# Five probability tiles and one run of value products a unit in a fused attention and expert kernel, with less space for values, inputs and splits and a new attention order

## The chip, the cores and the metric

The kernel runs on one core of a Trainium2 chip. Its engines each have their own instruction queue: TensorE (PE, with its weight loads shown apart as PEld), VectorE (DVE), ScalarE (ACT), GpSimd (POOL) and SyncE (SP), which issues most DMAs. The metric is the device time of one execution in microseconds, the median of three runs: 1045.88 us before the change (1041.61 to 1047.19).

## What is computed

One transformer layer on 2048 tokens of width 512: layer norm, attention with 32 heads of width 16 in which a query sees its last 256 keys, a residual, layer norm, and a mixture of 8 experts (hidden width 1376) of which each token takes its best two, with a second residual.

```python
qkv = (layernorm(x) @ wqkv).reshape(B, S, 3, H, Dh)         # H = 32, Dh = 16
scores = einsum("bhqd,bhkd->bhqk", q, k) * Dh ** -0.5
mask = (i - j >= 0) & (i - j < 256)
p = softmax(where(mask, scores, -1e9))
h = x + einsum("bhqk,bhkd->bhqd", p, v).reshape(B, S, D) @ wo
gates = softmax(layernorm(h) @ wg); top 2 of 8, weights made to sum to 1
out = h + sum over a token's two experts of weight * gelu(xn @ w1[e]) @ w2[e]
```

## The kernel before

**Numbers.** Matrices are multiplied in a fast 32-bit form. So that little is lost, an operand is split in a high and a low part (`split`: ACT rounds the high part, DVE or POOL takes the low part as the difference), and three products are added: high by high, high by low, low by high. One product of 512 inner rows by 512 columns is thus 12 matmuls.

**Attention.** The tokens are cut in 4 chunks of 512 (`c`), the heads in 8 groups of four (`g`). A unit `u = 8c + g` is one chunk of queries with one group of heads: 32 units. For a chunk, `norm_and_v` loads four blocks of x (pool `xn`), norms them (`rstd` on POOL), turns them on PE (line 592) and makes V (line 603). For a unit, `qk` loads a piece of the weights into a stage (`wst`), makes Q and K (line 660) and carries them through DRAM into one of four slots; `maxes` finds the largest score of each query (PE line 729, DVE line 734); `attend` makes the scores (line 778), exponentials (ACT, line 784), masks (POOL affine selects, line 810; in the last three units DVE does it before the exponential, line 754), and the products with V (line 834). `project` multiplies the finished chunk by `wo` (line 912, by way of the split buffer `ohl`), adds the residual, norms, turns (line 997), makes the gates (line 1004), and `route` (from line 1070) sends token numbers to a table in DRAM by eight small scatters on POOL (line 1101).

**Tiles of a unit.** A unit's scores fall in four tiles of key blocks, A (keys before the chunk, not in the first chunk), B, C and D. A tile's probabilities lie in one buffer of the pool `pt`, of which there are three. The V products of a tile use the array in four column strips of 32, one for each head (`tile_position=(0, 32 * j)`), where every other matmul uses the whole array. `ENDS` says after which tiles the V products of the tiles so far are made, in one run:

```python
ENDS = ("BCD", "BD", "BD", "ABCD")        # by chunk
```

So a unit of the first chunk has three runs, one of the second and third has two, one of the fourth has four.

**Experts.** Expert 0 begins with 384 early token rows, gathered when the third chunk's routes are in the table (POOL line 1315, turned by PE at line 1320), while the fourth chunk is projected and routed. Its remaining rows and experts 1 to 7 follow: up products (line 1347), gelu, down products (lines 1379 and 1422), and scatters that add to the output (line 1402).

**Order.** Nothing runs as written. Each step is a task with an engine, an estimated duration, a priority and the buffers it takes; `Plan.order` plays the tasks through with these estimates and so fixes each engine's instruction order. `SHIFT` moves the priority of a kind of task up or down, by stretch of the program; `SWITCH` is the estimate of what PE loses between whole-array matmuls and strips. On the chip every queue runs in the order given and waits where data are late.

Of the kernel before, what the change touches and what calls it, by code (L numbers as in the profile page):

```python
# [7 lines left out]
F32 = mybir.dt.float32  # L8
# [19 lines left out]
ENDS = ("BCD", "BD", "BD", "ABCD")  # L28
PVD = 770
LATE_MASKS = 8 * NC - 3  # L30
SWITCH = 95
# [29 lines left out]
    "maxes.halves.POOL": (0, -10.16, -12, -9.92, 0, 0, 0),  # L61
    "maxes.mm.PE": (-11.91, -7.13, 0.16, 0.06, 1.04, 0, 0),
    "norm_and_v.DVE1": (-1.2, 0, 0, -0.7, 0, 0, 0),
    "norm_and_v.SP1": (0, 0, -10.01, 0, 0, 0, 0),
    "norm_and_v.mm.PE": (0, 3.93, 3.16, 5.45, 0, 0, 0),
    "norm_and_v.turn.PE": (0, -12, -12, -8.6, 0, 0, 0),
    "part.DVE1": (0, 0, 0, 0, 0, 0.72, 0),
    "part.POOL1": (0, 0, 7.7, 0, 0, 0, 0),
    "part.mm.PE": (0, 0, 2.16, 0.86, 1.78, 0, 0),
# [1508 lines left out]
```

## Time and profile before

| | us |
|---|---|
| median of three runs | 1045.88 (1041.61 to 1047.19) |
| the profiled execution | 1048.93 |
| its span, first to last instruction | 1046.9 |
| PE busy | 1023.9 (98%) |
| PE weight loads busy | 844.0 (81%) |
| VectorE, GpSimd, ScalarE busy | 646.5, 626.7, 536.2 |

The attention units fill the trace from about 48 to 500 us, the fourth chunk's projection and routing lie beside expert 0 up to about 565, and the experts fill the rest. A row of the timeline gives start, length, engine, line, operation, tiles and how many equal instructions were merged; in brackets how long the engine was idle before and what ended that. A matmul's length includes its way through the array, so the next one starts earlier than that: what a matmul costs is read from start to start.

### The profile page before, as it was taken

The numbers are of one execution on the slowest core, as the hardware profiler recorded it, in microseconds if no ns is written. First come the engines' busy times: TensorE is split into PE (matmuls) and PEld (weight loads), VectorE is DVE, ScalarE is ACT, GpSimd is POOL, SyncE is SP. The second block draws the span as 40 slices with busy tenths as digits, with TensorE's granted clock in tenths as the row PEclk, the third lists the DMA queues.
The fourth block names the chain that finished last, engine by engine and source line by source line (L and its number), as shares of the span: only waits on it lengthen the run. The fifth ranks groups of instructions, "written<-read, shape, count | busy, mean of one in ns | idle before, by whom it ended". The sixth has DMA issues, their size and how long they took to land. (4 is left out here: it accounts for less than half of the span.)

```text
span 1046.9 us, 19919 instructions
## 1 busy us (share of the span) xinstructions
PE 1023.9 (98%) x6722; PEld 844.0 (81%) x6722; DVE 646.5 (62%) x1951; ACT 536.2 (51%) x1143; POOL 626.7 (60%) x986
## 2 busy tenths in 40 slices
PE   8999999999999999999899999999999999999997
PEld 5877778877777777755798898998999989878795
DVE  8988876887677777776752556354544545544440
ACT  3477747575666666567541554163362543525340
POOL 5687749777887858646496144187484673844111
PEclk9999999999999999988899999999999999999999
DMA  6999877769687868663526343164444544554522
GB/s 211 271 253 243 252 192 220 224 179 201 192 249 171 201 149 217 193 166 87 157 103 147 95 142 107 52 163 97 122 107 128 147 103 101 125 136 154 121 80 29
DMA packets 143887, 164.48 MB, mean 157 GB/s; under 512 B 68587, under 2 KB 86571, under 8 KB 143776
## 3 DMA queue, kind: packets, MB, share of 16 engines
q1 hardware_dynamic: 128448, 145.96, 49.5%
q0 software_dynamic: 15328, 17.16, 9.7%
q8 instruction: 55, 0.90, 0.3%
q14 instruction: 56, 0.46, 0.2%
HBM read 111.10 MB, written 51.43 MB: 155 GB/s over the span
## 5 line engine op out<-in xcount | busy, mean ns | idle before, releaser
L734 DVE CUSTOM_DVE_ANT_0 one<-one,masked 128x320 f32<-128x320 f32 (+4 forms) x512 | 230.3, 494 | 59.5 <-PE one L729 54.1
L1347 PE MATMUL one<-mr 128*128 128x288 f32 (+14 forms) x1716 | 255.2, 309 | 2.5 <-issue 1.2
L1347 PEld LDWEIGHTS one<-mr 128*128 128x128 f32 (+1 forms) x1716 | 243.2, 186 | 11.8 <-issue 1.6
L784 ACT ACTIVATE zone<-one 128x384 f32<-128x384 f32 (+1 forms) x480 | 208.3, 495 | 79.4 <-PE one L778 55.7
L810 POOL TENSOR_SCALAR_AFFINE_SELECT zone<-zone 128x256 f32<-128x256 f32 (+1 forms) x332 | 151.5, 481 | 59.8 <-ACT zone L784 53.4
L1379 PE MATMUL one<-zone,mr 128*128 128x512 f32 (+4 forms) x648 | 154.9, 394 | 0.0
L479 POOL TENSOR_TENSOR mr<-mf,mr 128x512 fp32r<-128x512 f32 (+4 forms) x99 | 123.9, 1263 | 48.8 <-ACT mr L475 47.6
L778 PE MATMUL one<-mr 98*128 98x384 f32 (+1 forms) x592 | 141.1, 331 | 3.3 <-ACT zone L784 1.7
L1379 PEld LDWEIGHTS one<-zone,mr 128*128 128x128 f32 (+4 forms) x648 | 117.1, 182 | 31.4
L778 PEld LDWEIGHTS one<-mr 98*128 98x128 f32 x592 | 97.6, 193 | 45.1 <-ACT zone L784 14.8
L475 ACT CAST mr<-mf 128x512 fp32r<-128x512 f32 (+6 forms) x152 | 108.4, 733 | 46.3 <-DMA mf<-in_A_wqk_dram 17.2
L1286 POOL DMA_INDIRECT mf<-xnd,mf x94 | 109.3, 1163 | 28.8 <-issue 27.7
L729 PE MATMUL one<-mr 96*128 96x320 f32 (+4 forms) x512 | 123.8, 318 | 0.6 <-DVE r_x L1062 0.3
L1402 POOL DMA_INDIRECT out_dram<-mf,tb x24 | 41.5, 1730 | 128.0 <-DVE mf L1390 114.7
L477 DVE TENSOR_TENSOR mr<-one,mr 128x512 fp32r<-128x512 f32 (+16 forms) x161 | 79.3, 509 | 57.6 <-ACT mr L475 43.7
L1361 ACT ACTIVATE one<-one 128x288 f32<-128x288 f32 (+13 forms) x132 | 54.8, 415 | 110.9 <-PE one L1347 91.6
L660 PE MATMUL one<-mr 128*128 128x512 f32 (+1 forms) x396 | 103.7, 389 | 2.3 <-ACT mr L475 2.0
L729 PEld LDWEIGHTS one<-mr 96*128 96x128 f32 x512 | 88.3, 191 | 21.3 <-DVE mx L734 10.2
L1402 POOL DMA_INDIRECT out_dram<-mf x40 | 65.2, 1630 | 63.0 <-DVE mf L1432 54.6
L834 PE MATMUL oT<-zone 128*17 128x384 f32 (+2 forms) x1408 | 96.9, 393 | 2.0 <-issue 1.4
L475 ACT CAST mr<-one 128x512 fp32r<-128x512 f32 (+16 forms) x161 | 70.7, 449 | 31.0 <-PE one L1320 16.9
L660 PEld LDWEIGHTS one<-mr 128*128 128x128 f32 x396 | 69.2, 189 | 14.0 <-ACT mr L475 3.5
(189 smaller groups left out, 1259.8 us busy)
## 6 DMA issues: line engine op xcount, KB each, us to landing
mf<-in_B_w_dram SPq DMA_DIRECT2D x32, 688.0 KB
mf<-in_B_w_dram SPq DMA_DIRECT2D x40, 512.0 KB
qkd<-mr SPq DMA_DIRECT2D x29, 512.0 KB
mr<-qkd SPq DMA_DIRECT2D x128, 96.0 KB
mr<-qkd SPq DMA_DIRECT2D x32, 384.0 KB
mf<-in_A_x_dram SPq DMA_DIRECT2D x32, 256.0 KB
mf<-in_A_wqk_dram SPq DMA_DIRECT2D x32, 256.0 KB
qkd<-mr SPq DMA_DIRECT2D x64, 128.0 KB
```

The source lines that it names most:

```text
L475: a = add("ACT", 51 + n * 0.86, lambda: nc.scalar.copy(dst_h(), src()), deps, prio, bufs)
L479: b = add("POOL", 60 + n * 2.3, lambda: nc.gpsimd.tensor_sub(dst_l(), src(), f32(dst_h())), [a], prio, bufs)
L660: nc.tensor.matmul(single[bk.h][:, s], wt()[:, int(i == 1), k * 128:(k + 1) * 128], xt[:, k, s], start=(i == 0 and k == 0), stop=(i == 2 a ...
L729: nc.tensor.matmul(view()[:, j], q_of(slot)[0:96, h + j, b].rearrange("p e q -> p (e q)"), K[slot.h][0:96, h + j, (b + k0) * 64:(b + 5) * ...
L734: nc.vector.tensor_tensor_reduce(v, v, masked[:, 320 - n:], scale=1.0, scalar=NEG, op0=OP.add, op1=OP.max, accum_out=mx_t[slot.h][:, h + j ...
L778: nc.tensor.matmul(single[bk.h][:, off:off + w], K[slot.h][0:98, h // 2, r * 128:(r + 1) * 128], q_of(slot)[0:98, h // 2, 2 * b:2 * b + 2 ...
L784: return add("ACT", 51 + n * 0.833, lambda: nc.scalar.activation(dst(), single[bk.h][:, 0:n].rearrange(order, **({"e": 2, "q": 64} if "e" ...
L810: nc.gpsimd.affine_select(v, v, pattern=[[0, v.shape[1]], [-1 if far else 1, 128]], compare_op=OP.is_gt if far else OP.is_ge, fill=0.0, ba ...
L1286: nc.gpsimd.indirect_dma_start(out=xg_t[i][:, t * 128:(t + 1) * 128], out_offset=None, in_=xnd4, in_offset=bass.IndirectOffsetOnAxis(ap=ql ...
L1347: nc.tensor.matmul(bank(), a[:, k, f * 128:f * 128 + w], spot[b][:, k, c0:c1], start=(i == 0), stop=(i == 11))
L1379: nc.tensor.matmul(single[bk.h][:n], h[a][:w], spot["w2"][2 * f + b][:w], start=(f == 0 and q == 0), stop=(f == NF - 1 and q == 2))
L1402: d = nc.gpsimd.indirect_dma_start(in_offset=None, compute_op=OP.add, **kw)
```

## The change

- **Tiles and runs.** `ENDS` goes. Units 0 to 27 make all their V products in one run after tile D; units 28 to 31 in two, after B and D. There are now four `pt` buffers, and one more (`pt_b`) that holds tile B of units 0 to 27 alone. It lies where two of the x blocks were.
- **Space.** V blocks go from ten to nine, so the V blocks numbered 11 and 15 may be written only when the last unit of the chunk before is done. The x blocks go from four to two after the first chunk, each pair with a `rstd` of its own. The weight stage `wst` and the split buffer `ohl` go from two to one.
- **Expert 0** keeps two of its hidden tiles in the region that attention leaves (`zone2`), and its weights also wait for the V products of unit 27.
- **Estimates and order.** `SWITCH` is 125 in place of 95, a gather 1260 ns in place of 950, and the table `SHIFT` is new throughout.

```diff
-ENDS = ("BCD", "BD", "BD", "ABCD")
+WHOLE = 8 * NC - 4
-SWITCH = 95
+SWITCH = 125
...
-    "norm_and_v.turn.PE": (0, -12, -12, -8.6, 0, 0, 0),
+    "norm_and_v.turn.PE": (0, -6.96, 0, -5, 0, 0, 0),
...
-    NQ, NPT, NV, NH, NN = 4, 3, 10, 3, 2
-    mr = consts.tile([128, 124 * KB], F32R, name="mr")
+    NQ, NPT, NV, NH, NN = 4, 4, 9, 3, 2
+    mr = consts.tile([128, 120 * KB], F32R, name="mr")
...
-    ohl = [(take(mr, 4, 128), take(mr, 4, 128)) for _ in range(2)]
+    ohl = [(take(mr, 4, 128), take(mr, 4, 128))]
-    xz = take(mf, 2048)
-    xn = [xz[:, i * 512:(i + 1) * 512] for i in range(4)]
+    xn = [take(mf, 512) for _ in range(2)]
     hl_f = take(mf, 512)
+    pt_z = take(mf, 2 * 768)
+    xn += [pt_z[:, i * 512:(i + 1) * 512] for i in range(2)]
+    wst = [take(mf, 512)]
...
-    plan = Plan(dict(xn=4, wgs=2, wst=2, hl=1, hl_more=1, qk=NQ, pt=NPT, osb=1, one=7, mx=3, ab=3, oT=1,
-                     h=NH, n=NN, nt=1, y=2, osl=1, ohl=2, ahead=4, tmp=2, xt=2, yq=1))
+    plan = Plan(dict(xn=2, xn_more=4, wgs=2, wst=1, hl=1, hl_more=1, qk=NQ, pt=NPT, pt_b=1, osb=1, one=7, mx=3, ab=3, oT=1,
+                     h=NH, n=NN, nt=1, y=2, osl=1, ohl=1, ahead=4, tmp=2, xt=2, yq=1))
...
-            if b == 3 or b == 1 and c == 0:
-                pair(*((b - 1, 2) if c == 0 else (0, 4)))
+            if b % 2:
+                pair(b - 1, 2)
...
-        ends, held, ready = ENDS[c], [], False
+        ends, held, ready = "D" if u < WHOLE else "BD", [], False
         for i, (name, parts) in enumerate(tiles):
             p = u + i / len(tiles)
-            pt = Buf("pt")
+            pt = Buf("pt_b" if name == "B" and u < WHOLE else "pt")
...
-        r1_free = qk_read[8 * NC - 1] + qk_read[8 * NC - 2] + v_done[NC - 1]
+        r1_free = qk_read[8 * NC - 1] + qk_read[8 * NC - 2] + v_done[NC - 1] + pv_last[WHOLE - 1]
```

Lines from 400 on have numbers one or two higher in the changed kernel: 780 are the scores, 731 the maxes, 836 the V products, 662 Q and K, 914 the projection, 1072 the routing, 1322 and 1349 expert 0's turns and up products.

**The runs, on PE.** Unit 0, before: its tile B and its tile C, each in a run of four matmuls (one for each head), with maxes (729) and scores (778) around them. `one` is a PSUM bank, `oT` the bank of the V products.

```order
L729 MATMUL one_75<-mr 128x320
L834 MATMUL oT<-zone 17x384 x4
L729 MATMUL one_77<-mr 128x320
L778 MATMUL one_79<-mr 128x256 x2
L778 MATMUL one_76<-mr 128x256
L729 MATMUL one_74<-mr 128x320
L834 MATMUL oT<-zone 17x384 x4
```

The same unit now, from its last score (the first row) to its only run:

```order
L780 MATMUL one_79<-mr 128x256
L662 MATMUL one_76<-mr 128x512 x4
L731 MATMUL one_80<-mr 128x320
L731 MATMUL one_75<-mr 128x320
L731 MATMUL one_74<-mr 128x320
L780 MATMUL one_78<-mr 128x384
L780 MATMUL one_79<-mr 128x384
L780 MATMUL one_77<-mr 128x384
L836 MATMUL oT<-mf,zone 17x384 x4
L836 MATMUL oT<-zone 17x384 x4
L836 MATMUL oT<-zone 17x128 x4
L836 MATMUL oT<-zone 17x256 x4
```

Tiles B, C and D (which has two parts) now stand in one row of strips, and four Q and K matmuls, three maxes and three scores of the next unit lie between the last score and the run.

**The routing of the third chunk, on PE.** Before, it stands ahead of the last run of unit 27:

```order
L834 MATMUL oT<-zone 17x384 x4
L778 MATMUL one_76<-mr 128x256
L778 MATMUL one_77<-mr 128x256 x2
L778 MATMUL one_80<-mr 128x256
L834 MATMUL oT<-zone 17x384 x4
L778 MATMUL one_74<-mr 128x256 x2
L778 MATMUL one_76<-mr 128x256
L778 MATMUL one_75<-mr 128x384
L1070 LDWEIGHTS before
L1070 MATMUL one_77<-r_m,before 128x32
```

Now it stands ahead of the last run of unit 29, among the first products of the fourth chunk's projection (914):

```order
L914 MATMUL one_80<-mr 128x512 x4
L780 MATMUL one_76<-mr 128x256 x2
L780 MATMUL one_74<-mr 128x384
L914 MATMUL one_80<-mr 128x512 x2
L780 MATMUL one_77<-mr 128x256
L731 MATMUL one_79<-mr 128x320
L780 MATMUL one_76<-mr 128x256 x2
L731 MATMUL one_78<-mr 128x320
L780 MATMUL one_74<-mr 128x256
L1072 LDWEIGHTS before
L1072 MATMUL one_77<-r_m,before 128x32
```

The third chunk's projection, turns and gates moved with it: 12 projection matmuls and all four turns and four gates of that chunk, which stood ahead of the last run of unit 27, now stand behind it.

**After the last run, on PE.** Before, behind the last V products of unit 31, the projection of four blocks (912) stands between the turns of expert 0's early rows (1320):

```order
L834 MATMUL oT<-zone 17x256 x4
L1320 MATMUL one_79<-ident,mf 128x128 x4
L1320 MATMUL one_74<-ident,mf 128x128 x4
L912 MATMUL one_75<-mr 128x512 x3
L912 MATMUL one_77<-mr 128x512 x3
L912 MATMUL one_80<-mr 128x512 x3
L912 MATMUL one_78<-mr 128x512 x3
L1320 MATMUL one_76<-ident,mf 128x128 x4
L1347 MATMUL one_79<-mr 128x384 x12
L1347 MATMUL one_74<-mr 128x384 x12
L912 MATMUL one_75<-mr 128x512 x2
```

Now:

```order
L836 MATMUL oT<-zone 17x256 x4
L914 MATMUL one_80<-mr 128x512 x3
L1322 MATMUL one_77<-ident,mf 128x128 x4
L914 MATMUL one_75<-mr 128x512 x3
L1322 MATMUL one_78<-ident,mf 128x128 x4
L914 MATMUL one_74<-mr 128x512 x3
L914 MATMUL one_79<-mr 128x512 x3
L1322 MATMUL one_76<-ident,mf 128x128 x4
L1349 MATMUL one_77<-mr 128x384 x12
L1349 MATMUL one_78<-mr 128x384 x12
L914 MATMUL one_80<-mr 128x512 x3
L1349 MATMUL one_76<-mr 128x384 x12
```

The products are the same in number. The pieces of three stand one by one between the turns, not four in a row, and behind the first two up products (1349) the last pieces follow with one up product between them.

## Rows read from the trace of the kernel before

**Rows 1.** The page's first part: busy time, share of the span and instructions of each engine.

```profile
PE 1023.9 (98%) x6722; PEld 844.0 (81%) x6722; DVE 646.5 (62%) x1951; ACT 536.2 (51%) x1143; POOL 626.7 (60%) x986
```

**Rows 2.** Busy time of each engine by stretch: the stretch and its length, then busy us and instructions of each engine, the granted share of PE's clock, the share of the DMA engines, GB/s.

```profile
100.00:450.00 350.00, 349.16 (x2667) 269.12 (x2665) 263.95 (x1015) 222.31 (x499) 257.60 (x498) 1.00 0.78 204
450.00:500.00 50.00, 45.62 (x291) 24.92 (x289) 35.25 (x131) 32.76 (x70) 29.90 (x43) 0.83 0.42 118
500.00:511.00 11.00, 8.42 (x27) 6.18 (x28) 6.49 (x11) 3.81 (x9) 3.93 (x3) 0.69 0.70 204
511.00:563.00 52.00, 52.00 (x291) 47.05 (x290) 29.67 (x105) 22.20 (x48) 40.58 (x64) 1.00 0.35 113
563.00:700.00 137.00, 133.47 (x895) 124.78 (x894) 66.36 (x116) 62.18 (x138) 53.60 (x62) 0.99 0.44 118
```

**Rows 3.** The timeline of PE around the first run of unit 0 (one tile; the trace counts two records for a matmul of line 834).

```profile
54.95 0.42 PE L729 MATMUL one<-mr 96*128 96x320 f32 x1
55.30 0.84 PE L834 MATMUL oT<-zone 128*17 128x384 f32 x8
56.07 0.41 PE L729 MATMUL one<-mr 96*128 96x320 f32 x1
56.32 0.52 PE L778 MATMUL one<-mr 98*128 98x256 f32 x3
```

**Rows 4.** The timeline of PE around a run of two tiles in the third chunk.

```profile
300.74 0.34 PE L778 MATMUL one<-mr 98*128 98x384 f32 x1
300.92 0.31 PE L729 MATMUL one<-mr 96*128 96x320 f32 x1
301.07 0.34 PE L778 MATMUL one<-mr 98*128 98x384 f32 x1
301.34 1.49 PE L834 MATMUL oT<-zone 128*17 128x256 f32 x24
302.76 0.41 PE L729 MATMUL one<-mr 96*128 96x320 f32 x1
303.01 0.40 PE L778 MATMUL one<-mr 98*128 98x256 f32 x2
```

**Rows 5.** What PE's idle time just before V products (line 834) waited for, over the whole trace: us, times.

```profile
  POOL zone L810: 5.0, 24
```

**Rows 6.** The timeline of the engines from the last score of unit 19 to its run.

```profile
324.71 0.64 PE L778 MATMUL one<-mr 98*128 98x256 f32 x4
325.03 1.17 ACT L784 ACTIVATE zone<-one 128x256 f32<-128x256 f32 x3 [0.43 <-PE one L778]
325.48 0.64 POOL L810 TENSOR_SCALAR_AFFINE_SELECT zone<-zone 128x512 f32<-128x512 f32 x1 [0.28 <-ACT zone L784]
326.58 1.49 PE L834 MATMUL oT<-zone 128*17 128x384 f32 x24
```

**Rows 7.** The same for unit 20, PE and POOL; the first of the three selects of the fourth row is the unit's last.

```profile
337.33 0.52 PE L778 MATMUL one<-mr 98*128 98x256 f32 x3
...
338.79 0.99 POOL L1101 DMA_INDIRECT table<-ent,si  x1 [0.15 <-issue]
...
340.25 1.82 POOL L810 TENSOR_SCALAR_AFFINE_SELECT zone<-zone 128x512 f32<-128x512 f32 x3
...
340.85 1.49 PE L834 MATMUL oT<-zone 128*17 128x384 f32 x24
```

**Rows 8.** The timeline of POOL, first and last of the six instructions of one root for four blocks.

```profile
136.72 0.25 POOL L486 TENSOR_SCALAR mv<-mv 128x4 f32<-128x4 f32 x1 [3.43 <-DVE mv L562]
...
139.02 0.20 POOL L494 TENSOR_TENSOR ry<-ry,mv 128x4 f32<-128x4 f32 x1
```

**Rows 9.** The timeline of PE: a turn and a gate of the third chunk, its routing, and rows of the last units.

```profile
433.26 0.60 PE L997 MATMUL one<-ident,mf 128*128 128x128 f32 x4
...
436.41 0.96 PE L1004 MATMUL one<-wgt,mf 128*128 128x8 f32 x8
...
445.56 0.19 PE L1070 MATMUL one<-r_m,before 128*128 128x32 bf16 x1
...
458.59 0.84 PE L834 MATMUL oT<-zone 128*17 128x256 f32 x16 [1.41 <-issue]
...
474.68 1.48 PE L834 MATMUL oT<-zone 128*17 128x128 f32 x16
```

**Rows 10.** From the third chunk's last scatter to expert 0's first up product: POOL, PE and ACT.

```profile
487.18 1.01 POOL L1101 DMA_INDIRECT table<-ent,si  x1 [0.15 <-issue]
...
497.37 1.01 POOL L1315 DMA_INDIRECT mf<-xnd,tb  x1 [1.17 <-DMA tb<-table]
...
498.92 0.83 PE L834 MATMUL oT<-zone 128*17 128x128 f32 x12 [0.57 <-ACT zone L784]
...
509.04 0.74 PE L1320 MATMUL one<-ident,mf 128*128 128x128 f32 x4 [0.29 <-DMA mf<-xnd,tb]
510.46 4.43 PE L1347 MATMUL one<-mr 128*128 128x384 f32 x24 [0.68 <-ACT mr L475]
```

**Rows 11.** The end of the fourth chunk's projection, and expert 0's first late rows, on PE.

```profile
514.72 0.62 PE L912 MATMUL one<-mr 128*128 128x512 f32 x2
...
520.30 1.55 PE L912 MATMUL one<-mr 128*128 128x512 f32 x6
...
565.13 0.75 PE L1320 MATMUL one<-ident,mf 128*128 128x128 f32 x4 [1.73 <-issue]
```

More of the change, by code (lines that the diff above doesn't have):

```diff
@@ L84 @@
-    "qk.rk.SP": (0, 0, 0, 0, -9.96, 0, 0),
-    "qk.rk_old.SP": (0, 4.37, -8.05, 4.93, 0, 0, 0),
[3 rows of a table removed]
-    "rstd.root.POOL": (-12, 0, 0, -4.65, 0, 0, 0),
-    "rstd_first.scale.DVE": (1.5, 0, 0, 0, 0, 0, 0),
-    "scores.ACT1": (0, -0.35, 10.68, 1.54, 1.92, 0, 0),
-    "scores.DVE1": (0, 0, 0, 0, 0, 4.66, 0),
-    "scores.mm.PE": (0, 0, -5.79, -0.07, 0.32, 0.07, 0),
[3 rows of a table removed]
+    "attend.mask.POOL": (0, -3.01, -3.39, -5.88, 0, 0, 0),
+    "attend.pv.PE": (0, 1.63, 0.01, 0.54, 0.79, 0, 0),
+    "clear.POOL1": (3.3, 0, 0, 0, 0, 0, 0),
@@ new lines @@
+    "consts_dve.DVE": (0, 6.36, 0, 0, 0, 0, 0),
+    "fill.rd_o.SP": (0, 0, -12, 0, 0, 0, 0),
+    "fill.rd_s.SP": (0, 0, 0, 2.44, 0, 0, 0),
[8 rows of a table added]
+    "maxes.halves.POOL": (0, -6.57, -2.72, -5.41, 0, 0, 0),
+    "maxes.mm.PE": (0, 0, 0.18, 0.08, 0.04, 0, 0),
+    "norm_and_v.DVE1": (3.11, 0, 0, 0, 0, 0, 0),
+    "norm_and_v.SP1": (-1.91, 0, 0, 0, 0, 0, 0),
+    "norm_and_v.mm.PE": (0, 4.1, 3.1, 5.63, 0, 0, 0),
+    "norm_and_v.turn.PE": (0, -6.96, 0, -5, 0, 0, 0),
+    "part.mm.PE": (0, 0, 2.16, 0, 1.94, 8.64, 0),
[3 rows of a table added]
@@ new lines @@
+    "project.gate.PE": (0, 0, 2.32, 0, 0, 0, 0),
+    "project.res.PE": (0, 0, 0, 0, 0, 12, 0),
+    "project.resid.DVE": (0, 0, 9.79, 0, 0, 0, 0),
+    "project.turn.PE": (0, 0, 1.56, 0, 3.41, -3.24, 0),
+    "qk.<genexpr>.<lambda>.SP": (0, 7.66, 3.6, 1.8, 5.3, 0, 0),
[4 rows of a table added]
+    "qk.mm.PE": (0, -1.5, -1.18, 0, 1.73, 0, 0),
+    "qk.rk.SP": (0, 1.42, 0, 8.4, 1.39, 0, 0),
+    "qk.rk_old.SP": (0, 0, 0, 7.87, 12, 0, 0),
[3 rows of a table added]
+    "rstd.root.POOL": (0, 0, -4.2, -6.05, 0, 0, 0),
+    "scores.ACT1": (0, -4.44, 0, 0, -5.94, 0, 0),
@@ L97 @@
+    "scores.DVE1": (0, 0, 0, 0, 3.25, 0, 0),
+    "scores.mm.PE": (0, 0, 0, 0.05, -0.15, -0.81, 0),
[3 rows of a table added]
     "turn_x.turn.PE": (0, 0, 0, 0, 0, 0, -6.53),
     "up.mm.PE": (0, 0, 0, 0, 0, 0, -10.65),
+    "weights_v.<genexpr>.<lambda>.POOL": (3.59, 0, 0, 0, 0, 0, 0),
 }
@@ L352, in retype @@
         zones.close()
-        z = zones.enter_context(tc.tile_pool(name="zone2", bufs=1)).tile([128, 36 * KB], F32R, name="zone2")
+        z = zones.enter_context(tc.tile_pool(name="zone2", bufs=1)).tile([128, 41 * KB], F32R, name="zone2")
         spot["w2"] = [take(z, 512) for _ in range(18)] + spot["w2"]
         at[id(mr)] = R4
-        while len(spot["h"]) < 2 * NF:
+        while len(spot["h"]) < 2 * NF - 2:
             spot["h"].append(take(mr, N))
+        spot["h"] += [take(z, N) for _ in range(2)]
     single = [psum.tile([128, 512], F32, name=f"one{i}", bufs=1) for i in range(7)]
@@ L494, in root @@
             nc.gpsimd.tensor_mul(yy, yy, vv)
-        return add("POOL", 1850 if n == 1 else 2450, root, deps, prio, bufs)
+        return add("POOL", {1: 1850, 2: 2050}.get(n, 2450), root, deps, prio, bufs)
     def rstd_first(v, y, deps, prio, n, i, first):
@@ L546, in norm_and_v @@
         p = 8.0 * c + -3.5 - 2.0
-        xb = [Buf("xn") for _ in range(4)]
+        xb = [Buf("xn_more" if c == 0 and b > 1 else "xn") for b in range(4)]
         if c == 0:
+            plan.free["xn_more"] = plan.free["xn_more"][2:]
             for b in xb:
-                b.h = plan.free["xn"].pop(0)[0]
+                b.h = plan.free[b.pool].pop(0)[0]
         mv = dict(v=mv_t[c % 2], y=ry_t[c % 2])
```

45 lines of the change are left out of this document (13 added, 32 removed), and 42 rows, old and new, of the table SHIFT.

## The prediction

> **What bounds the kernel now.** I read the page's engine shares first, then the stretches, then PE's timeline from start to start. PE is busy for 1023.9 of 1046.9 us [rows 1], and in the middle of attention, 100 to 450 us, for 349.16 of 350 [rows 2]; no other engine passes 264 of 350 there. But a matmul's shown length overlaps the next one, so a busy share proves little. The starts say more: in the third chunk a score matmul of 384 columns is followed after 0.18 us and a max of 320 columns after 0.15 us, while each is shown with over 0.3 us [rows 4]. They follow one another with no room between them, so in this stretch a gap that PE no longer makes shortens the kernel, unless a wait takes its place.
>
> From 450 to 511 us it is different. PE's weight loads are busy for 24.92 of 50 us against 269.12 of 350 before, the granted clock is 0.83 and then 0.69 on average, which means that part of the time ran at the lower level, 1.2 GHz, after PE had waited [rows 2], and PE waits before runs [rows 9]. There the last units are a chain from scores over DVE, ACT and back. From 511 us on PE is full again, with expert 0 beside the fourth chunk's end.
>
> **Runs of V products: the gain.** A run of one tile takes 0.77 us from its start to the next whole-array matmul (55.30 to 56.07) [rows 3]. A run of two takes 1.42 us (301.34 to 302.76) [rows 4]. Two of one thus cost 2 x 0.77 - 1.42 = 0.12 us more inside. Around the run two steps are long: into it 0.27 us (301.07 to 301.34) where the same score matmul otherwise takes 0.18, and behind it the max takes 0.25 us (302.76 to 303.01) where it otherwise takes 0.15 [rows 4]. So a run costs 0.12 + 0.09 + 0.10 = 0.31 us beyond its products; without the step behind it, which another cause could share, 0.21.
>
> The count comes from the two settings. First chunk: 8 units from 3 runs to 1, 16 fewer. Second and third: 16 units from 2 to 1, 16 fewer. Fourth: units 24 to 27 from 4 to 1, 12 fewer, units 28 to 31 from 4 to 2, 8 fewer. That is 52 of 88. The 44 in the units up to 27 lie where PE is full: 44 x 0.31 = **13.6 us** (9.2 by 0.21). The 8 in units 28 to 31 lie where PE waits anyway: between nothing and 8 x 0.31 = 2.5 us; I take the middle, **1.2**.
>
> The Trainium skill, Perfetto Trace Analysis, section "Identifying the Most-Contended Engine", says that matmul busy share is no good measure of how near TensorE is to its limit and that the weight loads' busy share should be read instead. By that PE would be at 77% from 100 to 450 us, something else could set the pace, and the gain would be lost; that is the first rival below, which has a chance of its own from rows.
>
> **Work moved into the last units.** The order puts 12 projection matmuls, four turns and four gates of the third chunk behind unit 27's last run, which stood ahead of it. A projection matmul goes by at about 0.23 us (a piece of six lasts 1.55 with its way out [rows 11]), so 12 are 2.8 us; a turn is shown with 0.60 and a gate with 0.96, so four of each are at most 4 x 1.56 = 6.2 [rows 9]. Some 8 us of PE's work leave a full stretch. In 450 to 500 us there is room for them: at the weight-load rate of the full stretch, 24.92 us of loads would fill 24.92 / 0.77 = 32 of the 50 us, so 18 are spare [rows 2]. It is worth between nothing, if it lengthens the chain there (DVE and POOL get the norms too, and DVE is busy 35.25 of 50), and 8 us. I take **2**, near the low end, because of the next but one paragraph.
>
> **New waits before a run.** One run now needs all four tiles. What is queued behind a run that waits is all of PE: maxes and so DVE, scores and so ACT. The bare way from the last score to its mask's end is 1.41 us: 324.71 for the score, 325.48 + 0.64 for the select [rows 6]. For unit 20 it took 3.56 us (337.33 to 340.89), since POOL, in order, had a scatter to send and a piece of the maxes in between, and the run began there and then [rows 7]. In the changed order, for unit 0, four matmuls of 512 columns, three maxes and three scores stand between: 4 x 0.23 + 3 x 0.15 + 3 x 0.18 = 1.9 us. That covers the bare way and not unit 20's. Before, runs waited 5.0 us for masks in 24 cases [rows 5], with 88 runs and more work between. For 28 runs the bounds are 0 and, if a quarter of them meet POOL as unit 20 did (3.56 - 1.9 = 1.7 us), 12 us. I take **2.5 us lost**, nearer to the 5.0 that was measured.
>
> **Less space.** Two x blocks bring a second root for each of three chunks. One root for four blocks takes 2.50 us of POOL (136.72 to 139.22) [rows 8]; one for two cannot take more, so POOL gets at most 3 x 2.5 = 7.5 us more in a stretch where it is busy 257.60 of 350 [rows 2]; its cover is that idle quarter, and the maxes and scores of units in flight cover PE's wait for the second pair of turns. I take **0.5 us** (0 to 3). V blocks 11 and 15 wait for the run of the last unit before, and one of seven PSUM banks is held for that time; the run is due anyway before the next unit's. The weight stage needs one load a unit, and units are some 14 us apart (runs at 326.58 and 340.85) [rows 6, 7]. Both at nothing, within the same 3 us. The added SP waits stand ahead of Q and K reads in the same queue, which belong to units two and more ahead.
>
> **The hand-over to expert 0.** The third chunk's routing moves from 445.56 to the last run of unit 29, which began at 474.68 [rows 9]. From there it needs eight scatters (8 x 1.01), 10.2 us from the last scatter to the first gather, 11.7 to the third turn and 1.4 to the up product [rows 10]: 31.4 us at best. From 474.68 to the last V products (498.92) there are 24.2 us, so expert 0 starts 7.2 us behind them at best; before it was 11.5 (510.46) [rows 10]. POOL has low parts of weights to make in between, so I take no change, with -4 to +8 as bounds; this is also why the spare room above is worth little. Behind that the one split buffer strings the last four pieces of the projection together: before they took from 514.72 to 521.9, and the late rows came 1.73 us late [rows 11]. One up product (half of 4.43 us [rows 10]) between pieces covers the split; at nothing, -1.7 to +4.
>
> **Sum.** -13.6 - 1.2 - 2 + 2.5 + 0.5 = -13.8 us. The profiled execution took 1048.93 us, so 1035.1; it lay 3.05 us above the median of the runs, so **1032** by the median.
>
> **Rivals.**
> 1. PE only looks full, and the pace is set by the loop of scores, exponentials, masks and slots. Then 44 gaps close and waits of the same size open, and only the 1.2 and 2 us remain: about 1043. For it speaks the 77% of the weight loads; against it the steps of 0.15 and 0.18 us, and an idle total of 0.84 us in 350 [rows 2, 4].
> 2. Slower: the run waits in lockstep. A run of four tiles keeps PE for about 2 x 1.42 - 0.12 = 2.7 us in which no score is made, and tile B of the next unit must wait until the run frees its one buffer. If every last mask then comes behind other POOL work as in unit 20, each of 28 runs waits 1.7 us: 47.6 us, against gains of 13.6 + 1.2 + 2 = 16.8, so 31 us more than before: 1077. It decides from 16.8 / 28 = 0.6 us a run. Against it: nearly three in four of the 88 runs did not wait for a mask at all [rows 5].
> 3. The routing comes too late, and PE stands idle behind the last run. At 10 us more it gives 1042, at the 8 and 4 us of the bounds together 1044.
>
> **Chances.** The forecast, between 1020 and 1040: 0.76. Rival 1: 0.10. Rival 2, in part or whole, slower than 1051: 0.08. Rival 3: 0.06, mostly within the bounds of no change. The lower end of the range takes all 8 us of the moved work, the whole 2.5 of the last eight runs and a hand-over 4 us sooner (-11.3); the upper end takes rivals 1 and 3. Range 1020 to 1046. A measurement of this kernel can tell about 0.5% from no change, that is 5.2 us. Faster than 1040.6: 0.76; within: 0.15; slower than 1051.1: 0.09.
>
> **What would show it.** Right: 36 runs; runs of four tiles of about 2.7 us; the last V products some 13 to 18 us earlier than 498.92; the same distance from there to expert 0's first up product; experts unchanged. Idle time of PE ahead of line 836 on POOL's selects, above 10 us in all, would show the waits mis-sized; PE idle ahead of lines 1322 or 1349 the hand-over; gaps ahead of the turns of a chunk (line 594) the x blocks.

## The result, and the profile after

| | before | after |
|---|---|---|
| median of nine runs on one chip, us | 1047.19 (1041.61 to 1049.31) | 1052.78 (1050.37 to 1058.82) |
| ratio, 95% interval | 1 | 1.0066 [1.0040, 1.0092] |
| profiled execution, us | 1048.93 | 1058.82, the slowest of its nine |
| its span, us | 1046.9 | 1056.9 |

The kernel became slower by 0.4 to 0.9%, where 1.3% faster was forecast. Two more sets of runs of the same kernel, each beside the kernel before on a chip of its own, gave 1.0071 [1.0043, 1.0099] and 1.0144 [1.0115, 1.0172] (runs again and again2 below). One execution of the run mid, 1108.44 us at a granted clock of 0.842, was in a slower state and is left out of mid's figures below.

The page's first part, as in [rows 1]: busy time, share and instructions of each engine.

```profile
PE 1021.2 (97%) x6722; PEld 857.7 (81%) x6722; DVE 649.5 (61%) x1951; ACT 536.7 (51%) x1143; POOL 633.6 (60%) x1003
```

The totals hardly move. The stretches of [rows 2] do; here are two of them, and below them five shorter ones: stretch and length, busy us (instructions) of PE, PEld, DVE, ACT and POOL, granted clock, DMA share, GB/s.

```profile
100.00:450.00 350.00, 343.68 (x2663) 273.82 (x2662) 265.18 (x1018) 228.62 (x512) 267.43 (x519) 0.98 0.77 209
450.00:500.00 50.00, 43.65 (x303) 29.41 (x301) 39.30 (x145) 25.91 (x57) 24.52 (x42) 0.86 0.40 117
...
20.00:60.00 40.00, 34.87 (x155) 28.07 (x154) 31.30 (x114) 13.23 (x26) 22.99 (x39) 0.93 0.87 225
260.00:280.00 20.00, 18.57 (x138) 14.18 (x134) 15.65 (x57) 10.19 (x24) 12.24 (x25) 0.91 0.61 156
335.00:350.00 15.00, 13.70 (x115) 10.37 (x107) 12.27 (x49) 9.43 (x23) 11.95 (x25) 0.89 0.50 156
365.00:380.00 15.00, 13.82 (x105) 10.88 (x102) 8.98 (x36) 10.71 (x25) 11.85 (x19) 0.89 0.79 215
390.00:405.00 15.00, 13.47 (x105) 10.48 (x101) 7.78 (x28) 9.03 (x20) 6.20 (x13) 0.89 0.63 133
```

The first of the five, before:

```profile
20.00:60.00 40.00, 39.66 (x201) 31.40 (x200) 36.48 (x131) 17.58 (x36) 30.57 (x51) 1.00 0.95 262
```

PE was full from 100 to 450 us before (349.16 of 350, clock 1.00). Now it is idle for 6.3 us there, in a few places, and around four of them the clock falls to 0.9. Before, the same five short stretches all had a clock of 1.00. These are the waits, on PE and then on the engines that it waited for (start, busy, engine, operation, count, idle time before and what ended it):

```profile
40.55 1.97 PE L662 MATMUL one<-mr 128*128 128x512 f32 x4 [2.56 <-ACT mr L476]
56.45 1.19 PE L662 MATMUL one<-mr 128*128 128x512 f32 x4 [1.83 <-ACT mr L476]
264.77 0.56 PE L731 MATMUL one<-mr 96*128 96x320 f32 x2 [1.44 <-DVE mx L736]
338.94 0.41 PE L731 MATMUL one<-mr 96*128 96x320 f32 x1 [1.29 <-DVE mx L736]
367.44 0.44 PE L780 MATMUL one<-mr 98*128 98x384 f32 x1 [1.18 <-ACT mf L786]
394.23 0.72 PE L731 MATMUL one<-mr 96*128 96x320 f32 x3 [1.53 <-DMA mr<-qkd]
```

```profile
39.88 0.62 ACT L476 CAST mr<-mf 128x512 fp32r<-128x512 f32 x1 [3.86 <-DMA mf<-in_A_wqk_dram]
261.54 0.70 DVE L563 BATCH_NORM_STATS2 s<-mf 128x6 f32<-128x512 f32 x1 [2.00 <-DMA mf<-in_A_x_dram]
366.41 0.59 ACT L851 COPY zone<-oT 128x512 f32<-128x512 f32 x1 [4.97 <-PE one L731]
```

None of the six is a run of V products. At 40 and 56 us a Q/K product waits for its weight tile, whose cast waited for the load into the one weight stage (3.86 us at 40). At 265 a max waits for VectorE, which stood 2.00 us at the statistics of an x block that had not landed. At 339 VectorE does routing steps of the second chunk first (336.77 to 338.35). At 367 the exponentials stand on ACT behind a copy of V products that itself waited 4.97 us. At 394 a read of old keys is late. The same four waits of the middle stand in both further profiles of this kernel: 0.96, 1.29, 1.17 and 2.72 us in again, 1.49, 1.28, 0.93 and 0.94 in again2. The waits of the run that were feared are smaller than before (5.0 us in 24 cases [rows 5]); of V products after:

```profile
  POOL zone L812: 1.8, 9
```

A run of four tiles, unit 18's, from its start to the next whole-array matmul 2.72 us (311.87 to 314.59):

```profile
311.87 0.84 PE L836 MATMUL oT<-zone 128*17 128x256 f32 x16
312.54 0.83 PE L836 MATMUL oT<-mf,zone 128*17 128x384 f32 x8
313.18 1.48 PE L836 MATMUL oT<-zone 128*17 128x384 f32 x24
314.59 0.97 PE L914 MATMUL one<-mr 128*128 128x512 f32 x3
```

The last units and the hand-over, PE (the answer to [rows 9, 10]; the first row is unit 27's run, L1072 the third chunk's routing, 508.16 the last V products):

```profile
442.84 0.84 PE L836 MATMUL oT<-zone 128*17 128x256 f32 x16
...
469.30 2.76 PE L836 MATMUL oT<-zone 128*17 128x256 f32 x24
...
482.09 0.18 PE L1072 MATMUL one<-r_m,before 128*128 128x32 bf16 x1 [0.44 <-ACT zone L786]
...
508.16 1.36 PE L836 MATMUL oT<-zone 128*17 128x128 f32 x12 [0.25 <-ACT zone L786]
...
516.67 0.75 PE L1322 MATMUL one<-ident,mf 128*128 128x128 f32 x4 [1.27 <-DMA mf<-xnd,tb]
518.09 0.95 PE L1349 MATMUL one<-mr 128*128 128x384 f32 x3 [0.68 <-ACT mr L476]
```

Unit 27's last run in the profile before:

```profile
446.32 0.84 PE L834 MATMUL oT<-zone 128*17 128x128 f32 x16
```

After, its only run, which holds all four tiles, begins at 442.84. With [rows 10] the difference of the spans splits into four:

| stretch | before | after | difference |
|---|---|---|---|
| start to unit 27's last run | 446.3 | 442.8 | -3.5 |
| from there to the last V products | 52.6 | 65.3 | +12.7 |
| from there to expert 0's first up product | 11.5 | 9.9 | -1.6 |
| from there to the end | 536.4 | 538.8 | +2.4 |

That sums to the +10.0 us between the spans. The first boundary is not quite the same place in both: the run after holds four tiles and takes 2.72 us (442.84 to 445.56), the run before holds tile D alone and takes 0.77 (446.32 to 447.09), so 2 us of V products stand ahead of the boundary before and behind it after. Two more profiles of the same kernel, in two of the runs below, have 534.9 and 537.8 in the last line, so 2.4 us there is within its scatter. Two questions are left: why the first stretch gained 3.5 us where the runs, the moved work and the boundary should have taken 13.6 + 8 + 2 out of it, and why the last units take 12.7 us longer.

### The profile page after: what moved, and what is told of

Same layout as the page of the kernel before. It is cut to its first block, busy times and chain, and to the rows that moved or that the text cites. A ratio compares the mean times of both kernels' runs of the same rounds, so it can differ in the third digit from the quotient of the medians.

```text
span 1056.9 us, 19831 instructions
## 1 busy us (share of the span) xinstructions
PE 1021.2 (97%) x6722; PEld 857.7 (81%) x6722; DVE 649.5 (61%) x1951; ACT 536.7 (51%) x1143; POOL 633.6 (60%) x1003
## 5 line engine op out<-in xcount | busy, mean ns | idle before, releaser
L736 DVE CUSTOM_DVE_ANT_0 one<-one,masked 128x320 f32<-128x320 f32 (+4 forms) x512 | 230.4, 493 | 69.4 <-PE one L731 65.5
L786 ACT ACTIVATE zone<-one 128x512 f32<-128x512 f32 (+2 forms) x368 | 161.2, 496 | 65.3 <-PE one L780 40.4
L480 POOL TENSOR_TENSOR mr<-mf,mr 128x512 fp32r<-128x512 f32 (+3 forms) x98 | 123.0, 1264 | 55.8 <-ACT mr L476 48.7
L731 PE MATMUL one<-mr 96*128 96x320 f32 (+4 forms) x512 | 134.8, 322 | 5.3 <-DVE mx L736 3.3
L812 POOL TENSOR_SCALAR_AFFINE_SELECT zone<-zone 128x256 f32<-128x256 f32 (+1 forms) x220 | 109.5, 520 | 24.0 <-ACT zone L786 23.3
L478 DVE TENSOR_TENSOR mr<-one,mr 128x512 fp32r<-128x512 f32 (+11 forms) x149 | 74.9, 513 | 77.2 <-ACT mr L476 61.1
L780 PEld LDWEIGHTS one<-mr 98*128 98x128 f32 x592 | 103.1, 196 | 23.0 <-ACT zone L786 9.8
L662 PE MATMUL one<-mr 128*128 128x512 f32 (+1 forms) x396 | 110.7, 408 | 6.4 <-ACT mr L476 5.6
L731 PEld LDWEIGHTS one<-mr 96*128 96x128 f32 x512 | 93.9, 194 | 25.8 <-DVE mx L736 5.5
L476 ACT CAST mr<-one 128x512 fp32r<-128x512 f32 (+11 forms) x149 | 66.7, 450 | 36.5 <-PE one L1322 19.8
L476 ACT CAST zone<-mf 128x512 fp32r<-128x512 f32 x73 | 42.9, 619 | 82.9 <-PE one L1424 47.2
```

Source lines behind the costliest of these rows:

```text
L476: a = add("ACT", 51 + n * 0.86, lambda: nc.scalar.copy(dst_h(), src()), deps, prio, bufs)
L480: b = add("POOL", 60 + n * 2.3, lambda: nc.gpsimd.tensor_sub(dst_l(), src(), f32(dst_h())), [a], prio, bufs)
L662: nc.tensor.matmul(single[bk.h][:, s], wt()[:, int(i == 1), k * 128:(k + 1) * 128], xt[:, k, s], start=(i == 0 and k == 0), stop=(i == 2 a ...
L731: nc.tensor.matmul(view()[:, j], q_of(slot)[0:96, h + j, b].rearrange("p e q -> p (e q)"), K[slot.h][0:96, h + j, (b + k0) * 64:(b + 5) * ...
L736: nc.vector.tensor_tensor_reduce(v, v, masked[:, 320 - n:], scale=1.0, scalar=NEG, op0=OP.add, op1=OP.max, accum_out=mx_t[slot.h][:, h + j ...
L780: nc.tensor.matmul(single[bk.h][:, off:off + w], K[slot.h][0:98, h // 2, r * 128:(r + 1) * 128], q_of(slot)[0:98, h // 2, 2 * b:2 * b + 2 ...
```

## The experiments

**Are runs worth what the sum says, or does PE only look full?** The run cut is the changed kernel with the runs of units 0 to 27 cut into single tiles again, spread among the matmuls ahead of the run in the same order, with everything else equal. Its trace has 112 runs, 76 more than the changed kernel's 36 (the expectation counts 74):

```
-            def pv(held=held, ready=ready):
-                for parts, pt, _ in held:
+            def pv(held=held, ready=ready, first=0, n=None):
+                for parts, pt, _ in held[first:n]:
...
     for t in order:
+        for pv, k in ahead.get(id(t), ()):
+            pv(first=k, n=k + 1)
         t.fn()
```

> The changed kernel in its own order and space, with the V products of units 0 to 27 cut into runs of one tile again: each piece ahead of the last stands before one of the whole-array matmuls that used to precede the run. 74 runs more, the same products. If a run costs what the prediction said (0.31 us), 74 x 0.31 = 23 us more than the changed kernel: 1076; by 0.21 us without the step behind it, 1068. If PE only looked full and closing its gaps opened waits (rival 1), the cuts cost little: under 1057. If long runs themselves starve VectorE and ScalarE, shorter runs would even be no slower than 1053.

1079.18 us (1074.73 to 1080.16), ratio 1.0319 [1.0288, 1.0350]. The changed kernel stood at 1.0066 to 1.0144, so 76 runs cost 18 to 26 us, **0.24 to 0.35 us each**. In the profiles unit 27's V products begin at 460.90 instead of 442.84. PE is no less busy from 100 to 450 us than in the changed kernel, and at a higher granted clock, but gets through 2514 matmuls there where the changed kernel gets through 2663:

```profile
100.00:450.00 350.00, 344.63 (x2514) 250.37 (x2517) 249.47 (x962) 216.90 (x483) 251.20 (x488) 1.00 0.74 197
```

PE's timeline shows a run of one tile as in [rows 3], 0.78 us from its start to the next max:

```profile
303.62 0.46 PE L732 MATMUL one<-mr 96*128 96x320 f32 x2
304.01 0.84 PE L837 MATMUL oT<-zone 128*17 128x256 f32 x16
304.79 0.41 PE L732 MATMUL one<-mr 96*128 96x320 f32 x1
```

So PE does set the pace, and the gaps are paid in full: the price of 0.31 us stands, and rival 1 falls.

**The waits in the middle: order or space?** Mid moves seven instructions of the order and changes nothing else: the x loads of the fourth chunk go earlier (their blocks were free), two routing steps of the second chunk behind the maxes, the copy behind the exponentials, and a read of old keys earlier. Each line names the instruction, its number, and what it now stands behind.

```
+MOVES = (
+    ("norm_and_v.SP1", 12, "maxes.SP1", 16),
+    ("norm_and_v.SP1", 13, "norm_and_v.SP1", 12),
+    ("route.s2b.DVE", 1, "maxes.DVE1", 357),
+    ("route.s4.DVE", 1, "maxes.DVE1", 358),
+    ("attend.ACT1", 21, "scores.ACT1", 327),
+    ("attend.SP1", 21, "attend.ACT1", 21),
+    ("qk.rk_old.SP", 18, "qk.<genexpr>.<lambda>.SP", 105),
+)
...
+    rearrange(plan, order, MOVES)
```

> The changed kernel in its own space with one stage, and seven instructions moved: two x loads of the fourth chunk 4 us sooner on SP, two steps of the second chunk's routing behind three maxes on VectorE, one copy of the V products behind four exponentials on ScalarE with its store, one read of old keys 7 us sooner on SP. If the four PE stalls of 1.2 to 1.7 us at 264.8, 338.9, 367.4 and 394.2 us are slips of an order that leaves no room, each with 1 to 2 us of lower clock behind it, PE gains 3.3 + 3.2 + 2.3 + 3.3 = 12 us: 1041. If the smaller space or the long runs are at fault, the stalls come back a little later: 1050 to 1053.

1054.12 us (1050.89 to 1057.22), ratio 1.0089 [1.0057, 1.0120], with no run of the changed kernel on that chip. So it was run beside one, mid2 beside again2:

> The changed kernel once more, as the yardstick beside the next two on one chip: 0.4 to 1.0% above the kernel before, with the four stalls of the middle at their places.

> The kernel mid once more beside the changed kernel. Its first profile was 6 us ahead of the changed kernel's at the end of the third chunk and 1 to 3 us at expert 0's start. If the stalls of the middle are worth 12 us at the end, 1.2% below again2; if what they give is given back in the last units and at the hand-over, 0 to 3 us below it.

Again2 1058.02 (1053.2 to 1061.24), ratio 1.0144 [1.0115, 1.0172]; mid2 1052.82 (1050.62 to 1054.56), ratio 1.0093 [1.0070, 1.0116]. By this pair the seven moves give back **5.3 us**, not 12. It is one pair: the two ratios of mid, 1.0089 and 1.0093, both lie between the 1.0066 and the 1.0144 of the changed kernel. What PE waited for from 60 to 440 us, the first three lines of again2 and then of mid2 (us, times, longest):

```profile
PE one L731 <- DVE mx L736: 3.6, 4, 1.5
PE one L731 <- ACT zone L613: 0.9, 1, 0.9
PE one L780 <- ACT zone L786: 0.9, 1, 0.9
```

```profile
PE one L802 <- ACT zone L808: 1.3, 2, 0.9
PE one L753 <- DVE mx L758: 1.3, 4, 0.6
PE one L753 <- ACT mf L808: 0.5, 1, 0.5
```

The longest wait goes, and short ones for ACT take part of its place: PE is idle there for 4.8 of 380 us in mid2, against 6.5 in again2 and 1.8 in the kernel before. So in part the waits came back elsewhere, which the expectation had named as the sign that space or long runs are at fault. The other side of a wait is the clock behind it. Fill leaves every wait in the order and puts 3 to 11 matmuls without use ahead of each of the six waiting instructions; again is the changed kernel beside it.

```
+FILL = (
+    ("qk.mm.PE", 15, 11),
+    ("qk.mm.PE", 21, 8),
+    ("maxes.mm.PE", 261, 6),
+    ("maxes.mm.PE", 327, 6),
+    ("scores.mm.PE", 327, 3),
+    ("maxes.mm.PE", 384, 6))
...
+        idle(fill.get(id(t), 0))
         t.fn()
```

> The changed kernel itself, as a yardstick beside the next three on the same chip, and for a second profile: by every theory 0.4 to 0.9% above the kernel before, 1048 to 1054. If the four stalls of the middle (264.8, 338.9, 367.4, 394.2 us) belong to the order, they stand in this profile too; if they are accidents of one execution, others stand there.

> The changed kernel with 3 to 11 matmuls without use (into the bank of the V products while it is empty) ahead of the six instructions before which PE waited: some 9 us of them, most of it in time that was idle. If much of a stall's price is the lower clock behind it, each of the six costs less: 5 to 9 us less than the changed kernel, about 1046. If the price is the wait alone, nothing is gained: 1053, or up to 1057 where a wait does not come and the filling does.

Again 1054.54 (1048.6 to 1060.87), ratio 1.0071 [1.0043, 1.0099]; fill 1054.16 (1048.71 to 1058.26), ratio 1.0048 [1.0025, 1.0071]: 2.4 us less by the ratios, half of the least expected, and 0.4 by the medians. The intervals overlap, so a gain in the total is not shown. The windows of the four middle waits, again and then fill:

```profile
255.00:275.00 20.00, 18.98 (x151) 14.19 (x154) 17.21 (x64) 12.20 (x27) 13.70 (x29) 1.00 0.74 212
330.00:345.00 15.00, 13.70 (x91) 10.95 (x83) 11.52 (x44) 8.63 (x21) 10.72 (x23) 0.77 0.50 154
360.00:375.00 15.00, 13.83 (x118) 10.39 (x114) 8.11 (x33) 8.93 (x21) 11.15 (x21) 0.89 0.85 207
385.00:400.00 15.00, 12.28 (x91) 9.48 (x90) 4.92 (x21) 6.94 (x18) 4.86 (x12) 0.89 0.64 148
```

```profile
255.00:275.00 20.00, 19.36 (x134) 14.27 (x134) 16.12 (x61) 11.78 (x28) 13.23 (x30) 1.00 0.81 204
330.00:345.00 15.00, 14.99 (x136) 10.71 (x138) 13.64 (x54) 10.79 (x26) 11.59 (x25) 1.00 0.63 182
360.00:375.00 15.00, 13.92 (x129) 10.03 (x122) 8.82 (x36) 10.11 (x24) 12.45 (x23) 1.00 0.73 203
385.00:400.00 15.00, 14.75 (x133) 10.50 (x126) 7.88 (x29) 9.21 (x21) 7.32 (x13) 1.00 0.82 168
```

In this profile, with PE kept at work, the clock stays at 1.00 through the same waits. In these two profiles unit 27's run begins at 442.00 (again) and 436.73 (fill), and expert 0's up product at 517.92 and 512.65: 5.3 us earlier at both, about the least that was expected. Behind that the experts took 539.9 us instead of 534.9, with the same instructions there (534.9 to 538.8 in the three profiles of the changed kernel), so the totals keep only part of it.

**The start: the one weight stage.** Stage2 gives the loads of units 1 to 8 a second stage (a buffer that is free at the start), so that they go out 6 to 7 us sooner:

```
+    wst.append(h_t[1])
...
+    for u in range(1, 9):
+        rw, ld, w = stage[u]
+        rw.h = u % 2 if u < 8 else 0
...
+        order.remove(ld)
...
+        order.insert(i, ld)
```

> The changed kernel with a second weight stage for units 1, 3, 5 and 7 alone (in a tile that stands empty until the first projection), so that the weight loads of units 1 to 8 go out 6 to 7 us sooner; every other instruction in its place. If the single stage makes PE wait at 40.6 and 56.5 us and the lower clock behind each wait is its price too, PE is 4 to 5 us less late by 80 us and the end moves with it: 1048. If the order of the start and not the stage is at fault, within 1 us of the changed kernel: 1053.

1056.17 us (1054.27 to 1058.42), ratio 1.0121 [1.0094, 1.0148]: no gain to be told at the end. Two windows, where the changed kernel has 34.87 busy at 0.93 in the first:

```profile
20.00:60.00 40.00, 36.74 (x200) 29.34 (x202) 34.26 (x127) 15.09 (x31) 24.95 (x44) 1.00 0.90 227
60.00:100.00 40.00, 37.88 (x258) 29.49 (x254) 29.89 (x132) 27.75 (x61) 30.41 (x54) 0.96 0.81 228
```

The stage's waits are gone, and in the next 40 us others come (2.1 us of idle PE, 0.25 in the changed kernel); that this part of the order was made for units that start later is a guess. Unit 27's run begins at 441.45, no earlier than in the changed kernel. With the seven moves as well, in two runs on two chips:

> Both of the last two: 1053 - 12 - 5 = 1036 if the five places are independent slips, which is below the kernel before (1047). If something else sets the pace, 1048 to 1053.

> The kernel mid_stage2 once more beside the changed kernel: by the sum of the slips 17 us below again2; if most is given back behind the third chunk, 3 to 8 us below it.

1051.08 (1046.52 to 1053.62), ratio 1.0071 [1.0045, 1.0098], and 1052.2 (1045.95 to 1055.68), ratio 1.0077 [1.0049, 1.0105]. Against again2 the second is 7.0 us faster, of 17 expected. Unit 27's run begins at 432.58 and 437.26 in their profiles, against 442.84, 442.00 and 439.65 in the three of the changed kernel: on average 6.6 us earlier. Mid alone has 436.25 and 438.92 there, 3.9 us earlier.

**The last units.** Four runs ask what holds them: PE's moved work, VectorE's masks in unit 29, both, or neither. Tail_pe makes PE's share larger, three residual products for one:

```
+                    for i in range(3):
+                        nc.tensor.matmul(single[bks[b].h], ident, h_t[xb.h], start=True, stop=i < 2)
```

> The changed kernel with each of the four residual products of the last chunk made three times (the first two are overwritten): 8 x 0.52 = 4.2 us more of PE's work between 472 and 494 us, nothing else. If PE has room in the last units, as the prediction had it, and VectorE sets their pace: 0 to 1.5 us more, 1053 to 1054. If PE's work there lies on the path: 4 us or, at the lower clock, up to 8 us more: 1057 to 1061.

Tail_dve leaves VectorE's masking of unit 29's scores out:

```
-lambda: hide(single[bk.h])
+lambda: hide(single[bk.h]) if u != LATE_MASKS else None
```

> The changed kernel without the masks that VectorE makes for unit 29, so that unit's products are those of unmasked scores (left out: 24 small operations of VectorE, some 9 us, between 460 and 485 us). If VectorE sets the pace of the last units, where the third chunk's norms and routing now stand among these masks, the last V products come 4 to 7 us sooner, and the end 2 to 7 us: 1046 to 1051. If the hand-over to expert 0 or PE sets it, 0 to 1 us: 1052 to 1053.

Tail_none leaves the third chunk's moved work behind unit 27's run out, and tail_both leaves out both:

```
+                        if lean and c == NC - 2 and (i, k) not in ((0, k0), (2, k1 - 1)):
+                            continue
...
+        if not (lean and id(t) in moved):
+            t.fn()
+        if t is pv_last[WHOLE - 1][0]:
+            lean.append(1)
```

> The changed kernel without what is left of the third chunk's projection behind unit 27's run (left out: three of four projection matmuls each, the multiplications, splits, residuals, norms, turns and gates; the routing reads older gates, so everything behind 510 us has other loads and is not compared). If this moved work pushes units 28 to 31 back by its own length, because it stands ahead of them in the queues and not in their gaps, the last V products come 52 to 56 us behind unit 27's run and not 65. If the chain of the last units itself needs that time, 62 to 65 us.

> As tail_none, and unit 29's masks left out as well: behind unit 27's run PE has some 8 us less to do, and VectorE some 15 us less. What comes behind 510 us has other loads and is not compared. If VectorE and the moved work together hold the last units back, their last V products come 52 to 57 us behind unit 27's run (kernel before: 52, changed: 65). If each queue finds the next late step, 60 to 63 us.

Where something is left out the routes differ, and times behind expert 0 can't be compared; so the measure is from unit 27's run to the start of the last run:

| run | us | what is changed |
|---|---|---|
| before | 51.0 | kernel before (446.32 to 497.31) |
| after, again, again2 | 64.0, 65.5, 63.9 | |
| tail_pe | 68.3 | 4.2 us more of PE |
| tail_dve | 64.9 | no masks in unit 29 |
| tail_none | 63.5 | moved work left out |
| tail_both | 55.3 | neither moved work nor masks in unit 29 |

In the six profiles of fill, stage2, mid, mid2 and both runs of mid_stage2, whose work in this stretch is the same as after, it took 61.5 to 66.5 us; that is its scatter. The ends of the last line:

```profile
442.56 0.85 PE L836 MATMUL oT<-zone 128*17 128x256 f32 x16
...
497.88 2.72 PE L836 MATMUL oT<-zone 128*17 128x384 f32 x24
```

Tail_none was expected at 52 to 56 if the moved work alone pushes, and tail_dve 4 to 7 us sooner if VectorE sets the pace; both fell. In tail_none PE stands idle instead: 11.2 us of 63.5 against 7.4 of 64.0 after. Each cause by itself hides the other; with both gone 9 us come back. Tail_pe, where nothing is left out, took 3 to 4 us more here than the three of the changed kernel, 2 us beyond the scatter, and got most of them back in the hand-over: 1055.71 us (1054.43 to 1062.7), ratio 1.0080 [1.0052, 1.0107], 0.9 us above again. So PE has no clear room here either. From unit 27's run to the last V products, before and after:

```profile
446.30:498.90 52.60, 48.49 (x321) 27.13 (x320) 38.01 (x143) 35.67 (x77) 31.00 (x47) 0.84 0.46 125
```

```profile
442.80:508.20 65.40, 57.79 (x438) 38.86 (x441) 52.39 (x195) 38.26 (x84) 37.87 (x63) 0.90 0.44 126
```

PE is busy for 9.3 us more and VectorE for 14.4. In the changed kernel's trace VectorE is busy 13.00 of the first 14.2 us of this stretch (10.54 before) and 11.06 of the next 12. The third chunk's routing steps on it begin at 469.04, and their last group at 482.78, 13.7 us; before they went from 441.23 to 446.27, 5.0 us. Rows of DVE after, and one of POOL:

```profile
468.13 3.27 POOL L480 TENSOR_TENSOR mr<-mf,mr 128x688 fp32r<-128x688 f32 x2 [9.39 <-ACT mr L476]
...
469.04 0.18 DVE L1049 TENSOR_REDUCE r_t<-lg 128x4 f32<-128x32 f32 x1
...
469.87 1.58 DVE L1051 TENSOR_TENSOR r_u<-r_u,e_rank 128x32 f32<-128x32 f32 x1
...
482.78 0.18 DVE L1093 TENSOR_TENSOR r_u<-one,e_pos 128x32 f32<-128x32 f32 x1
```

**Another order for both designs.** The table of numbers that sets the order was searched anew in one way for the changed kernel, the kernel before, and the changed kernel with two weight stages, with longer estimates for routing, norms and late transfers:

```
-        t.late = LATE.get(kind, 0)
+        t.late = LATE.get(kind, 0) + LATER.get(kind, 0)
+        t.dur += SLOWER.get(kind, 0)
```

> The changed kernel's tiles, runs and space with another order: a SHIFT table searched with longer estimates for the steps that ran late (routing, residual, x loads, old keys) and judged also with transfers that come up to 2 us late. If the slips of the order are what the change lost, the four stalls of the middle go and with them 8 to 12 us: 1040 to 1046, below the kernel before. If the space given up costs what the runs bring, no order helps: 1050 and more.

> The kernel before with its own tiles, runs and space, and an order searched in just the same way. If the runs are worth 13 us between equally good orders, this one is 8 to 13 us slower than after_re, and no faster than the kernel before, which had hardly a stall: 1045 to 1049. If runs and space cancel, it is within 4 us of after_re.

> As after_re, with a second weight stage for units 1, 3, 5 and 7 that the planner knows of. If the single stage cost the start 3 to 5 us, that much faster than after_re; if the order does, within 2 us of it.

1081.58 (1074.91 to 1086.61), ratio 1.0320 [1.0287, 1.0353]; 1063.16 (1057.93 to 1066.04), ratio 1.0141 [1.0112, 1.0170]; 1101.01 (1097.96 to 1102.23), ratio 1.0497 [1.0469, 1.0525]. All three lose. The table moved the experts too (547, 545 and 584 us from the first up product to the end, against 536), so the totals don't compare the designs; up to expert 0 the new tables stand at 525.95, 511.48 and 515.46 against 510.46 of the kernel before. After_re came out as it was to if no order helps, 1050 and more. Before_re was to be 8 to 13 us slower than after_re if the runs pay between equally good orders; it was 18 us faster, 14.5 up to expert 0. The second stage was to bring 3 to 5 us; up to expert 0 it brought 10.5, and the total lost. Whether the three searches came equally near to their best is not known. What this shows is that the kernel before, with another order and nothing else changed, moves by 1.4%, as much as the whole change or more. No version that was run beats the kernel before by its ratio.

## Why the prediction was wrong

**Runs of V products: the gain.** Right: 36 runs, four tiles in 2.72 us, 0.24 to 0.35 us a run against 0.31. By the rule of the Trainium skill that the prediction weighed (Perfetto Trace Analysis, "Identifying the Most-Contended Engine"), weight loads busy for 273.82 of 350 us, 78%, leave headroom. The cut says otherwise: the added gaps came through in full, and the steps of [rows 4] were the better witness. The last V products were to come 13 to 18 us earlier; they came 9.2 later (508.16 against 498.92), for the reasons that follow.

**New waits before a run.** The feared mechanism did not come: 1.8 us for masks against 5.0, so it is a small gain where 2.5 us of loss stood in the sum, and rival 2 falls.

**Less space.** This step failed at the start. "The weight stage needs one load a unit, and units are some 14 us apart" was read from the third chunk. In the first, units follow more closely (runs at 100.86, 110.11, 119.88, 128.83 and 138.30 us): 4.4 us of waits for two weight tiles, and 2.8 us more by the clock (0.93 in 40 us), 7.2 in all. Stage2 removes those waits, but alone it brought nothing by unit 27's run, so what the one stage costs is read from the trace and not shown by removal. The two x blocks hurt once, at 265 us, and there the load stood late in the order: mid sends it sooner, and that wait is gone.

**The sum had no term for the order.** This is the main failure ahead of unit 27's run. Costs were asked of the parts of the change; but a new order sets thousands of instructions anew, and four of them slipped, at 265, 339, 367 and 394 us, by 1.44 + 1.29 + 1.18 + 1.53 = 5.4 us. At the windows' clock that costs another 0.09 x 20 + 3 x 0.11 x 15 = 6.8. Together with the start that accounts for 19.4 us, about the 20 that are missing (13.6 + 8 + 2 - 3.5). PE's own account agrees: it was idle for 5.1 + 6.3 us in the stretches from 20 to 60 and from 100 to 450 us, where it had been idle for 0.3 + 0.8. So what the runs won was won, and was lost again as idle time and clock; that much the trace shows. That the order did it, and not the smaller space, is in part argued, since the waits at 40, 56 and 265 us are for space or loads as well, and most of the idle time of the middle stayed when the four were removed. By removal less is shown: mid gave 5.3 us, mid with the second stage 7.0, and fill 5.3 up to expert 0.

**Work moved into the last units.** Its sign was wrong: 2 us were to be won. The size of the work was right, 8 us. "There is room for them" was read off PE's weight loads and failed: the stretch grew by 12.7 us, 2 of which are the boundary, so it gave back all of the 8 and some 3 more. PE alone does not bound it, since leaving the moved work out gives nothing; it is a chain over DVE as well, as the prediction itself wrote, and the moved norms, the routing and unit 29's masks all go onto DVE. Tail_both shows that masks and moved work do it together; what the single share of each is can't be told, since leaving out one gives nothing.

**The hand-over to expert 0.** Right: -1.6 us, within -4 to +8. The routing's turn on PE came at 482.09, 36.0 us ahead of the up product against 31.4 at best, and PE waited 1.27 us for the third gather. But in again2 it waited 3.38 us for it, and expert 0's first up product stands at 518.09, 517.92 and 517.79 in the three profiles, though unit 27's run began at 442.84, 442.00 and 439.65. So rival 3 is a small part of the loss, and the hand-over takes up some of what is won ahead of it. The late projection pieces with one split buffer cost nothing that is visible beyond the scatter of the last line.

**What stays open.** Some 7 us of the 12 ascribed to the middle waits, and 10 of 17 with the start, did not come back when the waits were removed. In again2, the yardstick, the granted clock from 100 to 450 us was 1.00 and not 0.98, so most of the 6.8 us of clock was not lost there to begin with; part of the waits returns as short waits on ACT; and part goes in the hand-over, where mid2 waits for the third gather for 3.62 us:

```profile
514.28 0.80 PE L1344 MATMUL one<-ident,mf 128*128 128x128 f32 x4 [3.62 <-DMA mf<-xnd,tb]
```

Again2 has such a wait too (3.38 us), so the split is not settled. Nor is it whether the design (one run a unit, less space) would win with an order as good as the one before.

## What to carry to other kernels

A local gain can be real, tested and priced rightly, and still be lost in the order that comes with it: give a reshuffled order a term of its own, bounded by what a few slipped transfers cost with the clock behind them. Idle time on an engine that waits for others is not yet room; before moving work into such a stretch, ask which engine its chain goes over, and what the work puts on that one. When two causes hide each other, take both away before calling either innocent.

## What was not expected of the hardware

- A wait of PE of 1.2 to 1.5 us came with a granted clock of 0.89 to 0.91 over the 15 or 20 us around it, so that 5.4 us of waits go with 6.8 us of slower matmuls. It is not so each time: again waits 0.96 us at 262 us and keeps 1.00 there.
- With 3 to 11 matmuls without use ahead of each wait the clock stayed at 1.00 around all four of the middle (fill, one profile); without them, again2 shows 1.00 around three of these four waits and 0.89 around one, so the clock's part is not the same in each execution.
- VectorE's step of 128x32 elements at line 1051 took 1.58 us at 469.87, and the same one 0.65 at 473.12. Beside the first, GpSimd subtracted low parts at line 480 until 471.40, when the step was just ending; no run here tests whether that is the cause.
- Expert 0's first up product to the end took 534.9, 537.8 and 538.8 us in three profiles of one kernel, and the ratio of one pair of kernels was 1.0066, 1.0071 and 1.0144 in three sets of runs.
